# One statistics series and one transpose for two token blocks, two earlier broadcasts, and an earlier first split, in a linear-attention and MLP kernel

## The chip, the cores and the metric

The kernel runs on one core of a Trainium2 chip, as one program. The metric is the time of one execution on the device in microseconds (us); lower is better. All times below are of that core.

## What is computed

2048 tokens of width 640 go through a layer norm and then, side by side, through an attention and an MLP; both results are added to the input.

```python
def _layernorm(x, axis=-1, eps=1e-5):
    m = jnp.mean(x, axis=axis, keepdims=True)
    v = jnp.var(x, axis=axis, keepdims=True)
    return (x - m) / jnp.sqrt(v + eps)

def _A_ref(x, wqkv, w_phi, wo):            # 32 heads of 20
    qkv = (x @ wqkv) ...                    # q, k, v per head
    pq = jnp.einsum("bhsd,hdf->bhsf", q, w_phi)
    pk = jnp.einsum("bhsd,hdf->bhsf", k, w_phi)
    phi_q = jnp.concatenate([_softmax(pq), _softmax(-pq)], axis=-1)
    phi_k = jnp.concatenate([_softmax(pk), _softmax(-pk)], axis=-1)
    kv = jnp.einsum("bhsf,bhsd->bhfd", phi_k, v)
    z  = jnp.einsum("bhsf->bhf", phi_k)
    num = jnp.einsum("bhqf,bhfd->bhqd", phi_q, kv)
    den = jnp.einsum("bhqf,bhf->bhq", phi_q, z)[..., None] + 1e-6
    return (num / den) ... @ wo

def _B_ref(x, w1, b1, w2, b2):             # hidden width 1728
    y = _layernorm(x, axis=-1)
    h = _gelu(jnp.einsum("bsd,df->bsf", y, w1) + b1)
    return jnp.einsum("bsf,fd->bsd", h, w2) + b2

x = A_x
xn = _layernorm(x, axis=-1)
return x + _A_ref(xn, A_wqkv, A_w_phi, A_wo) + _B_ref(xn, B_w1, B_b1, B_w2, B_b2)
```

## The kernel before, in words

Every float32 operand of a matmul is split into a high and a low part (`split`, lines 53 and 54: ACT makes the high part by a copy, DVE or POOL subtracts it to get the low part), and a product is three matmuls (`mm3`, lines 60 to 62). The tokens are four blocks b of 512. The hidden width of the MLP is 14 chunks of 128, taken two at a time in seven groups g.

**A pass of the MLP** is one group for one block: `first` makes one hidden chunk by five `mm3` into a bank of the accumulator memory (banks 0, 1, 2 in turn), followed by the gelu (L242, ACT) and the split of its result (ACT L53, DVE L54, tile `m`). Then come five output chunks: ten matmuls or so each, into banks 5, 6, 7 in turn, each added to the tile `acc` by DVE (L286 in the first group, L288 after). Passes overlap by one: the two `first` of a pass stand ahead of the five output chunks of the pass before. Since three banks go round, an output chunk may start only when DVE has added up the chunk three places before it.

**Background work.** All else is written as Python generators that hang on `mlp.beside`: after each `mm3` (about 0.68 us of PE) one `next` lets the generator place a little more. So a count of `yield`s is a distance in PE's order. PE, DVE, ACT and POOL keep the order in which the program is written out in this part; the DMA issues on SP are ordered by a scheduler, and SP issues one after the other, waiting at each until its buffer or source is ready. The generator that matters here is `prep` (from line 448), which runs beside passes of blocks 0 and 1:

- twelve jobs of `prep_fold` (matmuls at L426 into banks 3 and 4 in turn, then a split) fold the feature map into the weights of k and q; six `yield`s each;
- among the jobs, `more_stats` (L434) makes mean and scale of the later tokens' eight tiles of 128: a tile `t` is loaded (L443, two buffers), two BN_STATS and a BN_AGGR on DVE (L126, L127), and after four tiles some small operations (L133 to L147) with one square root on ACT (L139), whose function table is loaded before it and gelu's again after it. On every second `yield` of a job, one step;
- five loads of v's weights (L465, buffers `raw`, two) with a split of each (tiles `wkh`, `wkl`);
- for b = 2 and then b = 3: `rows` (L166) copies the block's means and scales into `sc` (L169, L170), PE transposes it into 8 rows (L174), DVE copies that out (L176), it is stored to DRAM (L177) and read back as a broadcast to all partitions into the tile `m5` (L179, 512 KB). Then, five times, a piece of x (L478, buffer `raw`): POOL subtracts the mean (L488), DVE multiplies with the scale (L491), ACT makes the high part (L495), DVE the low part (L498), and both are stored (L500).

**The attention's end.** In the last group (g = 6) `first_split` (L931) splits the first block's attention output, `at[0].split` (ACT L914, DVE L916), for the output projection (L1020). It starts beside the pass (6, 3), after three empty `yield`s, and places one of its six steps per `yield`. The second chunk of group 6 is narrower and is built from halves: ACT L267, DVE L268, ACT L269 and L270, POOL L271.

## Time and profile before

| what | value |
|---|---|
| median of the runs; lowest | 741.25 us; 740.52 us |
| the profiled execution; its span | 740.65 us; 738.9 us |
| granted clock of TensorE | 1.000 |
| PE busy | 717.3 us, 97% of the span |
| DVE, ACT, POOL busy | 480.5, 314.4, 370.5 us |
| DMA, mean over the span | 129 GB/s |

In the rows of a timeline stand the start from the span's begin, the duration, engine, line, operation, the tiles written and read, the shapes, the count, and in brackets how long the engine had been idle before and what ended that. PE rows overlap: a matmul of 512 columns starts every 0.23 us and is shown 0.39 us long, so the bracket counts from a modelled end. In the chain of waits each piece is start, length, and what was waited for. In a table of windows the columns are the stretch, its length, the busy time of PE, PE's weight loads, DVE, ACT and POOL, the granted clock, the DMA share and GB/s.

### The profile page before, as it was taken

What the parts mean: (1) busy time and instruction counts of PE and PEld (TensorE: products, weight loads), DVE (VectorE), ACT (ScalarE), POOL (GpSimd) and SP (SyncE); (2) the same over time, 40 slices, a digit from 0 to 9 for tenths busy, and PEclk for the clock granted to TensorE, in tenths of its full rate; (3) what the DMA queues carried; (4) which work ended last, traced back from release to release, by engine and by line L of the source; (5) the groups of instructions that cost most, each with busy time, mean ns of one, the idle gap of its engine ahead of it and who ended that gap; (6) DMA issues with size and microseconds to landing.
All of it is one profiled execution on the core that took longest, in us unless ns stands there. A gap on an engine that the chain in (4) does not pass through costs nothing.

```text
span 738.9 us, 9634 instructions
## 1 busy us (share of the span) xinstructions
PE 717.3 (97%) x3423; PEld 606.6 (82%) x3423; DVE 480.5 (65%) x790; ACT 314.4 (43%) x518; POOL 370.5 (50%) x321
## 2 busy tenths in 40 slices
PE   4999999998999999999999999999999999999998
PEld 4888788777788998998998888888878888877886
DVE  7846744565653888888878788635565656766331
ACT  3614434333332455455345456246555556440110
POOL 1501222343321797697778889446576777304000
PEclk9999999999999999999999999999999999999999
DMA  9604467465543124634600705753433453153222
GB/s 333 214 8 121 146 170 183 133 198 149 166 167 142 64 80 161 149 101 161 143 0 1 179 0 200 179 162 111 125 110 115 118 154 92 48 209 129 86 84 73
DMA packets 64520, 95.36 MB, mean 129 GB/s; under 512 B 13312, under 2 KB 35216, under 8 KB 62848
## 3 DMA queue, kind: packets, MB, share of 16 engines
q1 hardware_dynamic: 64184, 94.74, 42.5%
q8 instruction: 27, 0.44, 0.2%
q14 instruction: 21, 0.17, 0.1%
q10 hardware_dynamic: 288, 0.01, 0.0%
HBM read 64.47 MB, written 30.26 MB: 128 GB/s over the span
## 4 chain that ended last, share of the span: by engine, by line
PE 79%; DVE 8%; DMA 5%; ACT 2%; issue 2%; POOL 2%; SPq 0%; POOLq 0%; DVEq 0%
PE bank L60 23%; PE bank L62 23%; PE bank L61 23%; PE bank L629 2%; PE bank L426 2%; PE bank L852 1%; PE bank L851 1%; DVE st L126 1%; DMA m<-r 1%; DVE y L916 1%; DMA raw<-in_wv 1%; DVE acc L288 1%; DVE xb L150 1%; POOL w L54 1%; POOL raw L488 1%
## 5 line engine op out<-in xcount | busy, mean ns | idle before, releaser
L54 POOL TENSOR_TENSOR w<-r,w 128x640 fp32r<-128x640 f32 x52 | 83.6, 1626 | 110.5 <-ACT w L53 104.6
L60 PE MATMUL bank<-y,w 128*128 128x512 f32 (+1 forms) x334 | 131.1, 392 | 0.9 <-ACT m L242 0.5
L62 PE MATMUL bank<-y,w 128*128 128x512 f32 (+1 forms) x334 | 129.8, 388 | 0.0
L61 PE MATMUL bank<-y,w 128*128 128x512 f32 (+1 forms) x334 | 129.6, 388 | 0.0
L60 PE MATMUL bank<-m,w 128*128 128x512 f32 x260 | 104.2, 401 | 4.2 <-DVE acc L288 3.9
L62 PE MATMUL bank<-m,w 128*128 128x512 f32 x260 | 101.9, 392 | 0.0
L61 PE MATMUL bank<-m,w 128*128 128x512 f32 x260 | 101.7, 391 | 0.0
L288 DVE TENSOR_TENSOR acc<-bank,acc 128x512 f32<-128x512 f32 x120 | 80.5, 681 | 16.5 <-PE bank L62 10.9
L60 PE MATMUL bank<-wkh,y 128*128 128x456 f32 (+2 forms) x240 | 88.6, 369 | 0.0
L61 PE MATMUL bank<-wkl,y 128*128 128x456 f32 (+2 forms) x240 | 88.5, 369 | 0.0
L62 PE MATMUL bank<-wkh,y 128*128 128x456 f32 (+2 forms) x240 | 88.4, 368 | 0.0
L54 DVE TENSOR_TENSOR m<-m,m 128x512 fp32r<-128x512 f32 (+1 forms) x54 | 42.7, 790 | 68.4 <-ACT m L53 68.4
L60 PEld LDWEIGHTS bank<-y,w 128*128 128x128 f32 x334 | 62.8, 188 | 14.1 <-DVE ob L1020 0.8
L62 PEld LDWEIGHTS bank<-y,w 128*128 128x128 f32 x334 | 62.7, 188 | 13.5 <-POOL w L54 0.4
L61 PEld LDWEIGHTS bank<-y,w 128*128 128x128 f32 x334 | 62.8, 188 | 12.7
L598 POOL TENSOR_TENSOR m<-m,mx 128x640 f32<-128x640 f32 (+2 forms) x48 | 44.4, 939 | 46.4 <-DVE mx L587 46.4
L580 ACT ACTIVATE m<-bank 128x456 f32<-128x456 f32 (+3 forms) x64 | 27.0, 421 | 95.0 <-PE bank L62 78.5
L60 PEld LDWEIGHTS bank<-m,w 128*128 128x128 f32 x260 | 48.9, 188 | 17.5 <-DVE acc L288 6.8
L845 POOL TENSOR_TENSOR e<-e,m 120x512 fp32r<-120x512 f32 (+1 forms) x28 | 38.0, 1358 | 43.0 <-ACT m L844 42.4
L62 PEld LDWEIGHTS bank<-m,w 128*128 128x128 f32 x260 | 48.8, 188 | 10.5
L601 DVE TENSOR_REDUCE sm<-m 128x64 f32<-128x1280 f32 x32 | 47.2, 1476 | 15.6 <-ACT m L599 15.5
L61 PEld LDWEIGHTS bank<-m,w 128*128 128x128 f32 x260 | 48.9, 188 | 9.6
(149 smaller groups left out, 1383.9 us busy)
## 6 DMA issues: line engine op xcount, KB each, us to landing
r<-in_w SPq DMA_DIRECT2D x52, 320.0 KB
e<-e SPq DMA_DIRECT2D x40, 240.0 KB
e<-acc SPq DMA_DIRECT2D x52, 160.0 KB
acc<-in_xT SPq DMA_DIRECT2D x4, 1280.0 KB
xb<-in_x SPq DMA_DIRECT2D x8, 320.0 KB
t<-in_x SPq DMA_DIRECT2D x8, 320.0 KB
raw<-in_xT SPq DMA_DIRECT2D x10, 256.0 KB
yh<-t SPq DMA_DIRECT2D x10, 256.0 KB
```

Source lines behind the costliest of these rows:

```text
L54: eng.tensor_tensor(lo, src, f(hi), op=ALU.subtract)
L60: nc.tensor.matmul(ps, lh, rh, start=first, stop=False, **kw)
L61: nc.tensor.matmul(ps, lh, rl, start=False, stop=False, **kw)
L62: nc.tensor.matmul(ps, ll, rh, start=False, stop=last, **kw)
L126: nc.vector.bn_stats(st[:, i, h, :], xb[:, h * 320:(h + 1) * 320])
L288: nc.vector.tensor_tensor(acc[b][:, m, :], pw, acc[b][:, m, :], op=ALU.add)
L426: nc.tensor.matmul(ps[:, i * kd:(i + 1) * kd], raw[:kk, (k + i) * P:(k + i + 1) * P], wpt[:kk, g, :kd // DF, 1:], start=True, stop=True)
L580: return nc.scalar.activation(p3[:, h:h + src.shape[1], 1:], src, AF.Copy).ins
L598: subs[n, t] = nc.gpsimd.tensor_tensor(ep[:, s], a, b, op=ALU.subtract)
L601: nc.vector.tensor_reduce(sm, e.rearrange("p s (h f) -> p (s h) f", f=DH), axis=AX, op=ALU.add)
L629: nc.tensor.matmul(kvp[g // 2][:VM, (g % 2) * 240:(g % 2) * 240 + 240].rearrange("p (s f) -> p s f", s=4), v[:, g * VS:g * VS + VM], ft[:, ...
L845: nc.gpsimd.tensor_tensor(pl, e, f(ph), op=ALU.subtract)
```

## The change

Four edits, all in generators beside the MLP. First, `more_stats` runs the eight later tiles as one series, with one square root, on every third `yield` of a job instead of every second. Second, `rows` is part of that series: the means and scales of both blocks go into one `sc` of 16 columns, with one transpose, one copy and one store. Third, the broadcast read is a function of its own, `load_rows`: for b = 2 it stands beside v's first load, for b = 3 at that block's start; the empty `yield`s ahead of the pieces become 5 and 10 (they were 2 and 7 for each block). Fourth, `first_split` loses its three empty `yield`s and places two steps per `yield`.

```diff
-    r_dram = [tc.dram_tile([8, P], F32, name=f"r{b}") for b in range(NB)]
+    r_dram = tc.dram_tile([2, 8, P], F32, name="r")
...
-    def rows(b, xp, ptile):
-
-        sc = xp.tile([P, 2, 4], F32, name="sc", bufs=1)
-        nc.vector.tensor_copy(sc[:, 0, :], mv[:, 4 * b:4 * b + 4, 0])
-        nc.vector.tensor_copy(sc[:, 1, :], ry[:, 4 * b:4 * b + 4])
-        for _ in range(2):
+    def rows(xp, ptile):
+
+        sc = xp.tile([P, 2, 2, 4], F32, name="sc", bufs=1)
+        for a, src in enumerate((mv[:, 8:16, 0], ry[:, 8:16])):
+            nc.vector.tensor_copy(sc[:, :, a, :], src.rearrange("p (b t) -> p b t", b=2))
+        for _ in range(5):
             yield
         ps = ptile()
-        nc.tensor.transpose(ps[:8, :P], sc.rearrange("p a t -> p (a t)"), idt)
-        sr = xp.tile([8, P], F32, name="sr8", bufs=1)
-        nc.vector.tensor_copy(sr, ps[:8, :P])
-        nc.sync.dma_start(r_dram[b], sr)
+        nc.tensor.transpose(ps[:16, :P], sc.rearrange("p b a t -> p (b a t)"), idt)
+        sr = xp.tile([16, P], F32, name="sr16", bufs=1)
+        nc.vector.tensor_copy(sr, ps[:16, :P])
+        nc.sync.dma_start(r_dram.rearrange("b r t -> (b r) t"), sr)
+
+    def load_rows(b):
+
         mr = mtile(5)
         nc.sync.dma_start(mr.rearrange("p a t -> p (a t)"),
-                          r_dram[b].rearrange("r t -> (r t)").unsqueeze(0).to_broadcast([P, 8 * P]))
+                          r_dram[b - 2].rearrange("r t -> (r t)").unsqueeze(0).to_broadcast([P, 8 * P]))
         return mr
...
     def more_stats():
 
-        for b in range(2, 4):
-            def tiles():
-                xbs = {}
-                for t in (*range(4 * b, 4 * b + 4), None):
-                    if t is not None:
-                        xbs[t] = fp.tile([P, 2, KC, G5], F32, name="t").rearrange("p a c f -> p (a c f)")[:, :D]
-                        nc.sync.dma_start(xbs[t], x[t * P:(t + 1) * P, :])
-                    if xbs and t != 4 * b:
-                        yield xbs.pop(min(xbs))
-            yield from stats(range(4 * b, 4 * b + 4), fp, tiles())
+        def tiles():
+            xbs = {}
+            for t in (*range(8, 16), None):
+                if t is not None:
+                    xbs[t] = fp.tile([P, 2, KC, G5], F32, name="t").rearrange("p a c f -> p (a c f)")[:, :D]
+                    nc.sync.dma_start(xbs[t], x[t * P:(t + 1) * P, :])
+                if xbs and t != 8:
+                    yield xbs.pop(min(xbs))
+        yield from stats(range(8, 16), fp, tiles())
+        for _ in range(2):
+            yield
+        yield from rows(fp, mlp.px)
...
-                if i > 0 and k % 2:
+                if i > 0 and k % 3 == 1:
                     next(more, None)
                 yield
...
+        for _ in more:
+            yield
         ahead = load_v(0)
+        mr = load_rows(2)
...
         for b in range(2, 4):
-            mr = yield from rows(b, fp, mlp.px)
             ahead = load(b, 0)
-            for _ in range(7):
+            if b == 3:
+                mr = load_rows(3)
+            for _ in range(5 if b == 2 else 10):
                 yield
...
     def first_split():
-        for i in range(3):
-            yield
         for c in range(KC + 1):
             at[0].split(c, nc.vector)
-            yield
+            if c % 2:
+                yield
```

How the order moves at three places of DVE, whose order is as written. The first is the ten output chunks of the two passes beside the jobs of k (`st` and `mv` are the statistics, `acc1` the sums of block 1, `bank5` to `bank7` the output banks, `wkl` a job's low part). Before:

```order
L286 SCALAR_TENSOR_TENSOR acc1_103<-bank6_723,b2t_61,acc1_103 128x512
L140 RECIPROCAL rr_746<-sr_745 128x8
L141 TENSOR_TENSOR rr_746<-rr_746,q_734 128x8
L142 TENSOR_TENSOR sr_745<-sr_745,rr_746 128x8
L143 RECIPROCAL ry_63<-sr_745 128x4
L286 SCALAR_TENSOR_TENSOR acc1_103<-bank7_738,b2t_61,acc1_103 128x512
L54 TENSOR_TENSOR wkl_593<-bank3_768,wkh_592 128x4x114
L146 RECIPROCAL ra_778<-sr_745 128x4
L147 TENSOR_TENSOR rs_all_64<-sr_745,ra_778 128x4
L126 BN_STATS st_781<-t_782 128x6 x2
L127 BN_AGGR mv_62<-st_781 128x2
L288 TENSOR_TENSOR acc1_103<-bank5_762,acc1_103 128x512
```

Changed:

```order
L289 SCALAR_TENSOR_TENSOR acc1_100<-bank6_717,b2t_61,acc1_100 128x512
L126 BN_STATS st_659<-t_711 128x6 x2
L127 BN_AGGR mv_62<-st_659 128x2
L289 SCALAR_TENSOR_TENSOR acc1_100<-bank7_729,b2t_61,acc1_100 128x512
L54 TENSOR_TENSOR wkl_590<-bank3_757,wkh_589 128x4x114
L126 BN_STATS st_659<-t_733 128x6 x2
L127 BN_AGGR mv_62<-st_659 128x2
L291 TENSOR_TENSOR acc1_100<-bank5_751,acc1_100 128x512
L54 TENSOR_TENSOR wkl_590<-bank4_780,wkh_589 128x114
L291 TENSOR_TENSOR acc1_100<-bank6_773,acc1_100 128x512
```

The small operations have left this stretch (they now stand behind the tenth chunk), and at most one tile's statistics stands between two sums.

The second place is behind v's last split (`wkl<-raw`), where the sums of block 0 (`acc0`) start; `m2` is the low part of a hidden chunk. Before:

```order
L54 TENSOR_TENSOR wkl_593<-raw_1237,wkh_592 128x640
L169 COPY sc_1266<-mv_62 128x4
L170 COPY sc_1266<-ry_63 128x4
L54 TENSOR_TENSOR m2_1245<-m4_1216,m2_1245 128x512
L176 COPY sr8_1281<-bank3_1279 8x128
L288 TENSOR_TENSOR acc0_102<-bank5_1272,acc0_102 128x512
```

Changed:

```order
L54 TENSOR_TENSOR wkl_590<-raw_1230,wkh_589 128x640
L54 TENSOR_TENSOR m2_1238<-m4_1209,m2_1238 128x512
L291 TENSOR_TENSOR acc0_99<-bank5_1264,acc0_99 128x512
L291 TENSOR_TENSOR acc0_99<-bank6_1272,acc0_99 128x512
L291 TENSOR_TENSOR acc0_99<-bank7_1280,acc0_99 128x512
L500 TENSOR_TENSOR raw_1259<-raw_1259,m5_1172 128x512
```

The copies into `sc` and the one out of the transpose's bank are gone from here, and the first piece of x for b = 2 comes two sums earlier.

The third place is the attention's first split (`y10<-ob0`) in group 6; `acc2` and `acc3` are the sums of blocks 2 and 3, `m4` the narrow chunk. Before:

```order
L288 TENSOR_TENSOR acc3_4089<-bank7_5799,acc3_4089 128x512
L916 TENSOR_TENSOR y10_5832<-ob0_4346,y00_5831 128x512
L54 TENSOR_TENSOR m1_5816<-m4_5815,m1_5816 128x512
L268 TENSOR_TENSOR m4_5815<-bank2_5844,m4_5815 64x512
L916 TENSOR_TENSOR y10_5832<-ob0_4346,y00_5831 128x512
L288 TENSOR_TENSOR acc2_4088<-bank5_5860,acc2_4088 128x512
L916 TENSOR_TENSOR y10_5832<-ob0_4346,y00_5831 128x512
L288 TENSOR_TENSOR acc2_4088<-bank6_5870,acc2_4088 128x512
```

Changed:

```order
L291 TENSOR_TENSOR acc3_4064<-bank7_5774,acc3_4064 128x512
L925 TENSOR_TENSOR y10_5797<-ob0_4321,y00_5796 128x512 x5
L54 TENSOR_TENSOR m1_5791<-m4_5790,m1_5791 128x512
L271 TENSOR_TENSOR m4_5790<-bank2_5828,m4_5790 64x512
L291 TENSOR_TENSOR acc2_4063<-bank5_5844,acc2_4063 128x512
L291 TENSOR_TENSOR acc2_4063<-bank6_5852,acc2_4063 128x512
```

All five low parts now stand ahead of the hidden chunk's, and none between the sums; on ACT the five high parts stand ahead of that chunk's gelu in the same way.

On SP two things move: the broadcast for b = 2 is issued just ahead of v's first load (it stood behind the first two loads of x's pieces), and the one for b = 3 stands ahead of the last stores of b = 2, where it waits for DVE's last multiplication with the old `m5`. On PE one transpose of the two is left, between two `mm3` of the tenth job.

## The prediction

> **What bounds the kernel now.** I read the table of windows first, to see whether PE has idle time at all and where.
>
> ```profile
> 60.00:90.00 30.00, 29.09 (x152) 23.79 (x151) 23.20 (x62) 11.92 (x23) 6.18 (x4) 1.00 0.55 161
> ...
> 126.00:150.00 24.00, 22.79 (x101) 18.25 (x100) 14.95 (x21) 9.78 (x15) 8.44 (x6) 1.00 0.50 156
> 150.00:200.00 50.00, 47.31 (x206) 37.95 (x205) 30.67 (x46) 16.99 (x27) 21.30 (x14) 1.00 0.58 171
> 200.00:640.00 440.00, 439.07 (x2108) 377.69 (x2108) 311.06 (x473) 218.89 (x350) 303.51 (x275) 1.00 0.39 115
> 640.00:680.00 40.00, 38.75 (x170) 31.16 (x169) 27.88 (x43) 10.96 (x19) 10.08 (x7) 1.00 0.40 143
> ```
>
> PE sets the pace: in the 440 us from 200 to 640 it is idle for 0.93 us, and its clock is granted in full in every row. What is left to win lies in 60 to 90 (0.91 us idle), 126 to 200 (1.21 + 2.69) and 640 to 680 (1.25), which are the places that the change touches. PE's timeline shows these stalls one by one; for the largest, I keep its neighbours.
>
> ```profile
> 70.53 0.47 PE L60 MATMUL bank<-m,w 128*128 128x512 f32 x1 [0.23 <-DVE acc L286]
> 76.72 0.50 PE L60 MATMUL bank<-m,w 128*128 128x512 f32 x1 [0.68 <-DVE acc L288]
> 132.26 0.39 PE L62 MATMUL bank<-m,w 128*128 128x512 f32 x1
> 133.83 0.27 PE L174 MATMUL bank<-idt,sc 128*8 128x128 f32 x1 [1.19 <-DVE sc L170]
> 134.17 0.40 PE L61 MATMUL bank<-m,w 128*128 128x512 f32 x1
> 164.73 0.50 PE L60 MATMUL bank<-m,w 128*128 128x512 f32 x1 [0.34 <-DVE acc L288]
> 168.74 0.27 PE L174 MATMUL bank<-idt,sc 128*8 128x128 f32 x1 [0.32 <-DVE sc L170]
> 178.63 0.39 PE L61 MATMUL bank<-m,w 128*128 128x512 f32 x1
> 178.85 0.39 PE L62 MATMUL bank<-m,w 128*128 128x512 f32 x1
> 180.87 0.50 PE L60 MATMUL bank<-m,w 128*128 128x512 f32 x1 [1.63 <-DVE acc L288]
> 181.21 0.40 PE L61 MATMUL bank<-m,w 128*128 128x512 f32 x1
> 195.15 0.50 PE L60 MATMUL bank<-m,w 128*128 128x512 f32 x1 [0.39 <-DVE acc L288]
> 659.27 0.50 PE L60 MATMUL bank<-m,w 128*128 128x512 f32 x1 [0.87 <-DVE acc L288]
> 677.10 0.50 PE L60 MATMUL bank<-y,w 128*128 128x512 f32 x1 [0.38 <-DVE ob L1020]
> ```
>
> The bracket understates a stall, since matmuls overlap. Undisturbed, they start 0.225 us apart (178.63 to 178.85). From 178.85 to 181.21 are two steps, 2.36 us in place of 0.45: a loss of 1.91 for an idle time of 1.63. So a stall costs its bracket plus 0.28; 132.26 to 134.17 gives the same (1.46 against 1.19 + 0.28). The losses are then 0.51, 0.96, 1.47, 0.62, 0.60, 1.91, 0.67, 1.15 and 0.66: 8.55 us, of which the change can reach all but the last, 7.9. That is 1.1% of the time, so whatever happens here stays within the 2% (14.8 us) that a measurement of this kernel can tell from no change.
>
> **The change part by part. The statistics.**
>
> ```profile
> 66.44 0.89 DVE L126 BATCH_NORM_STATS2 st<-t 128x6 f32<-128x320 f32 x2 [0.45 <-DMA t<-in_x]
> ...
> 73.73 1.35 DVE L147 TENSOR_TENSOR rs_all<-sr,ra 128x4 f32<-128x4 f32 x1
> ...
> 76.03 0.64 DVE L288 TENSOR_TENSOR acc<-bank,acc 128x512 f32<-128x512 f32 x1
> ```
>
> Ten output chunks stand here in a row, three to a stretch of two jobs' halves, about 5.3 us of PE. DVE's part of such a stretch is three sums (0.6 each), a job's low parts (0.9) and, before, three tiles' statistics (1.05 each with the BN_AGGR): 5.85 us, more than PE takes, plus waits for the tile's load and the small operations in between. With two tiles' statistics it is 4.8 us. A sum may be late by two chunks, some 3.5 us, so DVE then keeps up and both stalls go: 1.47. I take 1.2 (bounds: 1.47, and 0.5 if only the first goes), because one of the later x tiles' loads now stands on SP behind weight loads that wait for POOL and can come late by a microsecond; a sum behind it has two chunks to spare, the low parts of the next job have less. One square root for two saves a handful of operations of 0.16 to 0.2 us on DVE, which nothing waits for.
>
> ```profile
> 69.22 1.28 ACT L139 ACT_TABLE_LOAD   x1
> ...
> 101.44 0.68 DVE L288 TENSOR_TENSOR acc<-bank,acc 128x512 f32<-128x512 f32 x1
> ```
>
> The table load moves, it does not go: there are two as before. One, 1.28 us, now stands ahead of a gelu near 90 us. That hidden chunk is first used by the pass whose sums start at 101.44, so ten microseconds hide it; without that cover it would cost its 1.28.
>
> **The transpose.**
>
> ```profile
> 132.71 0.82 DVE L54 TENSOR_TENSOR wkl<-raw,wkh 128x640 fp32r<-128x640 f32 x1 [1.02 <-ACT wkh L53]
> ...
> 133.53 0.16 DVE L170 COPY sc<-ry 128x4 f32<-128x4 f32 x1
> ...
> 134.76 0.67 DVE L288 TENSOR_TENSOR acc<-bank,acc 128x512 f32<-128x512 f32 x1
> ```
>
> PE stood at 133.83 because `sc` waits in DVE's order behind v's last split, which waits for ACT and that for a DMA. In the changed order the copies into `sc` stand five `yield`s' steps, over ten microseconds, ahead of the transpose, so this wait goes. What is late next: the first sum, at 134.76. Without the copy out of the transpose it starts at about 134.6 and ends at 135.25, while PE, not held up, wants its bank three chunks (18 steps, 4.08 us) after this pass's first matmul at 131.13 (132.26 is the sixth), at 135.2. So a wait of about 0.1 with its 0.28 stays: of 1.47 I take 1.1 (bounds: 1.47, and 0.5 if v's loads come 0.6 later). The second transpose's 0.60 goes; the one that is left costs 133.83 to 134.17 less one step, 0.11, at another place: 0.5 in sum.
>
> ```profile
> 113.15 0.33 SPq L465 DMA_DIRECT2D raw<-in_wv  x1
> ...
> 118.94 0.73 ACT L53 ACTIVATE wkh<-raw 128x640 fp32r<-128x640 f32 x1
> ...
> 172.16 4.56 DMA m<-r
> ```
>
> The broadcast is issued ahead of v's first load. That load has 5.8 us until its split. If it had to wait for a whole broadcast, the 4.56 us from issue to landing in this chain of waits, on top of about 3 for itself, it would come some 2 us late, and the DVE half of that split stands behind three sums until 122 us, which hides it. Cost nothing; two microseconds on ACT if it does not hide.
>
> **The broadcasts of x's pieces.**
>
> ```profile
> 164.59 0.68 DVE raw L491
> ...
> 169.41 2.73 DMA r<-sr
> ...
> 178.39 1.28 POOL raw L488
> ```
>
> ```profile
> 178.46 1.75 DVE L491 TENSOR_TENSOR raw<-raw,m 128x512 f32<-128x512 f32 x1 [1.18 <-POOL raw L488]
> 180.14 1.27 DVE L288 TENSOR_TENSOR acc<-bank,acc 128x512 f32<-128x512 f32 x2
> ```
>
> For b = 3 the store and the read back take 2.73 + 4.56 = 7.3 us behind the transpose; POOL can only then subtract, DVE's multiplication waits, and behind it stand the two sums that PE waits for at 180.87. Now the store is done 50 us ahead, and the read is issued when the last multiplication of b = 2 has freed the old `m5`. That one runs at 164.59 now, so even with no gain ahead of it the broadcast lands by 165.3 + 4.6 = 169.9, seven us before it does today. The 1.91 goes whole (bounds: 1.91, and 0.6 if a held multiplication still adds a microsecond there, as 178.46 shows). For b = 2 the pieces start some 4 us sooner, so that DVE's work on the fourth piece no longer falls late ahead of the sum that PE waits for at 164.73: of 0.62 I take 0.5. The stall at 195.15 comes from a low part that met a POOL operation; such a meeting moves rather than goes, and of 0.67 I take 0.3 (bounds for the two: all 1.29, or a loss of 0.6 if a pass that is free today gets such a meeting).
>
> **The first split.**
>
> ```profile
> 651.69 0.69 ACT L242 ACTIVATE m<-bank,b1t 128x512 f32<-128x512 f32 x1 [6.49 <-PE bank L62]
> ...
> 656.60 4.26 ACT L914 ACTIVATE y<-ob 128x512 fp32r<-128x512 f32 x8
> ```
>
> ```profile
> 657.25 1.36 DVE L916 TENSOR_TENSOR y<-ob,y 128x512 fp32r<-128x512 f32 x1 [0.78 <-ACT y L914]
> 658.53 0.68 DVE L288 TENSOR_TENSOR acc<-bank,acc 128x512 f32<-128x512 f32 x1
> ```
>
> The third high part stands on ACT behind the narrow chunk's last copy, so DVE's low part waits for it 0.78 us, and the second sum behind it comes at 658.53, which is PE's stall at 659.27. Now ACT makes all five (0.53 each) in the 6.49 us that it idles ahead of the gelu at 651.69, and DVE the five low parts, 0.6 each, behind the last sum of the pass before, ahead of 652; the gelu's own low part is not due before 653 (651.69 + 0.69 + 0.63 for the copy). Were that gap not there, the five would put the gelu off by 2.7 us. The second sum then comes at about 656.4. Of 1.15 I take 1.1 (bounds: 1.15 and 0.6, if the second sum is late by half of what it is now). What follows (the shuffles and low parts up to 677) hangs in DVE's order behind sums that PE paces, so it moves with PE and its 0.66 stays.
>
> **The sum.** 1.2 + 1.1 + 0.5 + 0.5 + 1.9 + 0.3 + 1.1 = 6.6, less 0.4 for meetings of DVE and POOL at new places: 6.2. From the profiled execution's own 740.65 that gives 734.5 us. It lies 0.6 below the median of the runs, so against that it is 0.9%.
>
> **The rivals.** First, a wait takes the place of the one removed: v's five splits are a chain of loads into two buffers, and PE, which now arrives 1.5 us earlier, stands at the first sum behind them, or the late x tile keeps one of the first two stalls. Then 1.0 is lost of the 1.2, 0.8 of the 1.6, and another 0.9 where the pieces of x follow v's loads: 737.2. For it speaks the 0.1 us margin above; against it that the broadcast has left the place where those loads run.
>
> Second, the stalls merely move on: if the background is itself the limit between 120 and 200, PE waits as long as before, a little later. Only 1.2 and 1.1 stay: 738.4. Against it, DVE is busy for 30.67 us of the 50 and POOL for 21.30.
>
> Third, slower than before: DVE and POOL hold each other up.
>
> ```profile
> 71.95 3.10 POOL L54 TENSOR_TENSOR w<-r,w 128x640 fp32r<-128x640 f32 x2 [35.43 <-ACT w L53]
> ```
>
> The tiny operation at 73.73 lasts 1.35 us and ends at 75.08, just where POOL's pair ends (75.05). Pieces that start earlier could meet POOL ahead of the first sum of each pass. That sum has about 1.4 us to spare (0.8 with a piece's operation ahead of it). Two held operations, each lengthened by up to 1.2 (the excess at 73.73), make 2.4 - 0.8 + 0.28, about 1.9 us a pass. Of my 6.2, the 2.7 of the three sum stalls (164 to 195) would go with it, leaving 3.5; so two of the five passes with pieces make it slower than before, and three give 740.65 - 3.5 + 5.7 = 742.9. For it speak 178.46 (1.75 in place of 0.68); against it, that it takes two such meetings in one pass, which only one of today's stalls (164.73) comes near. The Trainium skill has this as a rule (SBUF — State Buffer, "SBUF: two separate sides"): VectorE and GpSimd share a pair of ports, taken as a whole by whichever instruction starts first, and an operation of DVE with two inputs from SBUF waits for all of a GpSimd instruction that reads SBUF. The end at 75.08 agrees with it; by the rule every meeting costs the rest of POOL's operation, which is this rival, while by the rows most operations pass untouched.
>
> **How the numbers follow.** The forecast has 0.70, the first rival 0.16, the second 0.07, the slower one 0.04; 0.03 is left for more than forecast (all 7.9 and some of the last stall: 732.2). The predicted time is 734.5. The range reaches from 732.0 to 738.2, which leaves out most of the second rival and the slower one. The cases all lie within 2%: faster by more than that would need 14.8 us where PE idles 7; slower by as much needs more held passes than there are. Faster 0.01, same 0.98, slower 0.01.
>
> **What would show it.** PE's waits for `sc` are gone; no wait of 1 us for `acc` near 180; the wait at 659 is gone and the one at 677 stays near 0.4; 60 to 90 and 126 to 200 show PE idle for less than 1.2 us together; PE's span elsewhere is unchanged. Wrong would be a new wait of PE behind v's splits, DVE waiting for `t<-in_x` again with a bank wait behind it, or multiplications L500 of 1.5 us and more ahead of a first sum.

## The result and the profile after

The changed kernel takes 734.13 us (median of six runs, 732.96 to 736.36), the kernel before beside it 741.02 (median of six): a ratio of 0.9911, 95% interval 0.990 to 0.9921, so 0.9% faster. Forecast were 734.5 and a range of 732.0 to 738.2. The profiled execution took 732.96 us with a span of 731.2 (before: 740.65 and 738.9); it is the fastest of the six, which matters below. Three single runs were disturbed (891.73 and 3005.81 of the kernel before, 1022.29 of the kernel with the broadcast behind v's third load, at a granted clock of 0.66): the ratios leave them out, the medians given do not, and without them 741.02 would be 740.8 and that later kernel's 733.0 would be 732.63.

The table of windows of the changed kernel, cut at the same times (columns: the stretch, its length, then busy time and instructions of PE, its weight loads, DVE, ACT and POOL, granted clock, share of the DMA engines, GB/s; the share counts a packet's whole time where it starts, so it can pass 1):

```profile
60.00:90.00 30.00, 30.00 (x159) 25.10 (x158) 21.18 (x55) 12.22 (x22) 6.17 (x4) 1.00 0.54 159
...
126.00:150.00 24.00, 23.49 (x104) 19.10 (x103) 15.53 (x21) 10.44 (x16) 9.07 (x7) 1.00 0.53 169
150.00:200.00 50.00, 50.00 (x222) 41.42 (x221) 30.70 (x46) 20.10 (x32) 20.73 (x15) 1.00 0.57 169
200.00:640.00 440.00, 439.03 (x2109) 377.60 (x2108) 309.53 (x470) 220.01 (x353) 302.87 (x274) 1.00 0.39 115
640.00:680.00 40.00, 39.63 (x175) 32.51 (x174) 26.87 (x42) 9.14 (x17) 8.80 (x6) 1.00 0.48 169
```

PE's idle time is now 0.00 in 60 to 90 (0.91 before), 0.51 and 0.00 in 126 to 200 (1.21 and 2.69), and 0.37 in 640 to 680 (1.25). The 440 us between have 0.97 against 0.93: the rest of the kernel is as it was. PE's timeline of the changed kernel shows the two stalls that these numbers stand for:

```profile
134.45 0.50 PE L60 MATMUL bank<-m,w 128*128 128x512 f32 x1 [0.51 <-DVE acc L291]
...
669.53 0.50 PE L60 MATMUL bank<-y,w 128*128 128x512 f32 x1 [0.37 <-DVE ob L1028]
```

Eight stalls have gone, one is new (134.45), and the one that the change could not reach is still there (677.10 before, 0.38). With 0.28 for each stall beside its bracket, the eight cost 0.51 + 0.96 + 1.47 + 0.62 + 0.60 + 1.91 + 0.67 + 1.15 = 7.89, the new one 0.51 + 0.28 = 0.79, and the transpose that is left 0.1: 7.0 of the 7.7 by which the span fell. Of the other 0.7, some 0.3 lies in the first and last microseconds, which the change does not touch; 0.4 I can't place.

The new stall's chain of waits in the changed kernel (start, length, what; each line was waited for by the next, and pieces called issue, of 0.02 to 0.04 us, are left out):

```profile
120.98 0.83 DVE wkl L54
121.83 4.74 DMA raw<-in_wv
126.59 0.75 ACT wkh L53
127.36 0.84 DVE wkl L54
128.22 2.85 DMA raw<-in_wv
131.09 0.74 ACT wkh L53
131.83 0.59 ACT m L245
132.44 0.64 ACT m L53
133.10 0.69 DVE m L54
133.80 0.61 DVE acc L291
134.45 0.50 PE bank L60
```

This is the chain of v's loads through two buffers: v's first split on DVE frees a buffer, the third load lands 4.74 us after its issue, its split frees the buffer for the fifth load, and behind that load's high part stand, on ACT, the gelu and high part of a hidden chunk, whose low part DVE makes just ahead of its first sum. In the kernel before, the same load took 3.93 us. This difference is what the later experiments look into.

### The profile page after: what moved, and what is told of

It is laid out like the page before. It is cut to its first block, busy times and chain, and to the rows that moved or that the text cites. A ratio compares the mean times of both kernels' runs of the same rounds, so it can differ in the third digit from the quotient of the medians.

```text
span 731.2 us, 9616 instructions
## 1 busy us (share of the span) xinstructions
PE 714.9 (98%) x3422; PEld 607.0 (83%) x3422; DVE 474.4 (65%) x779; ACT 314.9 (43%) x517; POOL 370.1 (51%) x321
## 4 chain that ended last, share of the span: by engine, by line
PE 84%; DVE 8%; POOL 2%; DMA 2%; ACT 2%; issue 1%; SPq 1%; DVEq 0%; POOLq 0%; ACTq 0%
PE bank L60 25%; PE bank L61 25%; PE bank L62 25%; PE bank L429 2%; PE bank L638 2%; POOL m L607 2%; PE bank L861 1%; PE bank L860 1%; DMA raw<-in_wv 1%; SPq L671 1%; DVE st L126 1%; DVE y L925 1%; DVE xb L150 1%; POOL m L618 1%; PE bank L268 1%
## 5 line engine op out<-in xcount | busy, mean ns | idle before, releaser
L245 ACT ACTIVATE m<-bank,b1t 128x512 f32<-128x512 f32 (+1 forms) x54 | 36.1, 671 | 53.6 <-PE bank L62 52.5
L60 PEld LDWEIGHTS bank<-m,w 128*128 128x128 f32 x260 | 48.9, 188 | 11.7 <-DVE acc L291 1.8
L62 PEld LDWEIGHTS bank<-m,w 128*128 128x128 f32 x260 | 48.8, 188 | 10.5
```

What stands on the lines that cost most here:

```text
L60: nc.tensor.matmul(ps, lh, rh, start=first, stop=False, **kw)
L62: nc.tensor.matmul(ps, ll, rh, start=False, stop=last, **kw)
L245: nc.scalar.activation(gt[:, cols], pz, AF.Gelu_apprx_tanh, bias=b1t[:, 2 * g + j:2 * g + j + 1])
```

## The experiments

Each kernel is shown as a difference to the changed kernel, or to the kernel before where that is said. The kernel before, run on the same chips, had medians of 741.14 to 741.35.

**The statistics' pace, alone.** The kernel before with one line changed.

```
-                if i > 0 and k % 2:
+                if i > 0 and k % 3 == 1:
```

> The kernel before with one edit: the statistics step on every third yield of a job instead of every second; two series, two transposes, two stores and reads as before. Theory (each stall its own cause): the waits at 70 and 77 us go (0.23 and 0.68 us idle, 1.47 us of time); the waits for the transposes and the one of 1.6 us near 180 stay within 0.3 us; 1.2 to 1.5 us under the kernel before. Rival (DVE's relief in the first part is what lets all that follows run on time): the later waits shrink by half or more as well, 3 us or more under the kernel before.

Measured: 739.38 us, ratio 0.9973 (0.9963 to 0.9984); PE's stalls at 70 and 77 are gone, and all later ones are still there (1.45 for `sc`, 1.63 at 180, 0.87 at 658 among them). So the later stalls don't hang on this one, and none of them shrinks: two are larger than before (1.45 in place of 1.19, and 0.54 in place of 0.34 at 163.83) and one of 0.25 for `w` is new (142.33). The edit gave 2.0 by the medians (1.2 to 2.7 by the interval) and 0.9 by the profiled spans, against my 1.2.

**The pace, undone.** The changed kernel with `k % 2`, everything else kept.

> The changed kernel with the statistics at every second yield again, as before the change, but in their one series. This tests the step of my prediction that the two stalls at 70 and 77 us go because DVE has one tile's statistics less per stretch of three output chunks (4.8 us in place of 5.85, against PE's 5.3). Theory: the pace is the cause; PE waits for sums between 60 and 90 come back, 0.5 to 1.0 us in one or two, and the time is 0.8 to 1.5 above the changed kernel's 734.1. Rival: what counted was that the square root, the reciprocals and the second table load no longer stand in this stretch; then 60 to 90 stays free of waits and the time is that of the changed kernel.

Measured: 735.95 us, ratio 0.9929 (0.991 to 0.9948), 1.8 above the changed kernel where 0.8 to 1.5 was expected. PE's timeline of this kernel between 60 and 90:

```profile
70.48 0.47 PE L60 MATMUL bank<-m,w 128*128 128x512 f32 x1 [0.29 <-DVE acc L289]
75.42 0.50 PE L60 MATMUL bank<-m,w 128*128 128x512 f32 x1 [0.82 <-DVE acc L289]
77.55 0.50 PE L60 MATMUL bank<-m,w 128*128 128x512 f32 x1 [0.46 <-DVE acc L291]
```

And DVE's, ahead of the second:

```profile
70.44 0.87 DVE L126 BATCH_NORM_STATS2 st<-t 128x6 f32<-128x320 f32 x2
71.34 0.21 DVE L127 BATCH_NORM_AGGREGATE mv<-st 128x2 f32<-128x12 f32 x1
71.47 0.70 DVE L289 SCALAR_TENSOR_TENSOR acc<-bank,b2t,acc 128x512 f32<-128x512 f32 x1
73.62 0.89 DVE L126 BATCH_NORM_STATS2 st<-t 128x6 f32<-128x320 f32 x2 [1.45 <-DMA t<-in_x]
74.54 0.21 DVE L127 BATCH_NORM_AGGREGATE mv<-st 128x2 f32<-128x12 f32 x1
74.67 0.70 DVE L289 SCALAR_TENSOR_TENSOR acc<-bank,b2t,acc 128x512 f32<-128x512 f32 x1
```

The stalls are back, 0.29 + 0.82 + 0.46 and 0.28 each, 2.4 us. The rival, that the square root's small operations were the cause, has fallen: in this kernel they stand behind the last of the three stalls (from 79.24 on). But the second stall shows that it is not DVE's sum of work alone. The statistics also arrive ahead of their tiles, and 1.45 us of waiting for `t<-in_x` stands in DVE's order ahead of the sum that PE needs. The slower pace cures both: in the changed kernel the only such wait is 0.31 (at 78.51), with no stall behind it. A second thing differs in this kernel: the statistics are done sooner, so b = 2's broadcast is issued at 96.13, 18.5 us ahead of v's first load (114.64), and PE waits 0.02 us behind v's last split. That will matter below.

**The first split, alone.** The kernel before with the new `first_split`.

```
-        for i in range(3):
-            yield
         for c in range(KC + 1):
             at[0].split(c, nc.vector)
-            yield
+            if c % 2:
+                yield
```

> The kernel before with the new first split alone. Theory (every stall has its own cause, and their losses add): only the wait of PE at 659 us goes, 0.87 us idle and 1.15 us of time, and the five others of 0.23 to 1.63 us between 70 and 196 us stay as they are; the time is 1.0 to 1.3 us under the kernel before. Rival (the early part frees the late one, the first split is hidden anyway): no difference, 0 to 0.3 us.

Measured: 739.7 us, ratio 0.9984 (0.997 to 0.9999). The stall at 659 is gone, all others remain; 1.6 by the medians (0.1 to 2.2 by the interval), against 1.15 that the stall cost. This agrees with terms that add up, but the interval is wide, and the profiled execution (743.14) is the slowest of the ten, with two waits that the profile before lacks (0.46 at 145.83, 1.43 at 423.32).

**The broadcast for b = 3, late.** The changed kernel, its means and scales for b = 3 stored and read back only in place, by a copy on DVE six yields behind the first load of x (the lines of `load_rows` that make this copy, store and read are left out here); the pieces start after 14 yields. The control has the early broadcast and the same 14 yields.

```
             if b == 3:
-                mr = load_rows(3)
-            for _ in range(5 if b == 2 else 10):
+                for _ in range(6):
+                    yield
+                mr = load_rows(3, late=True)
+            for _ in range(5 if b == 2 else 8):
```

> The changed kernel, but the store and the broadcast read of block 3's means and scales hang on an extra small copy on DVE six yields into the block, and its pieces start after 14 yields instead of 10, so that copy, sums and the first multiplication stand in the order that the kernel before has there. Theory (the wait near 180 us came from the store and read of 7.3 us): PE waits again for a sum, 1.0 to 1.7 us idle near 173 us, 1.3 to 2.0 us more than the same with an early read. Rival (it is the place of the first multiplication ahead of the sums, and not the read, that made the wait): no more than 0.3 us over the control with 14 yields.

> Control for the late read: the changed kernel with 14 yields instead of 10 ahead of block 3's pieces, broadcast early as in the change. Theory: the multiplication finds its operand, no wait of over 0.5 us near 173 us, time within 0.7 us of the changed kernel. Rival (the place alone makes the wait): 1.0 to 1.7 us idle there and 1.3 to 2.0 us over the changed kernel.

Measured: 736.03 us (ratio 0.9925, 0.9901 to 0.995) with the late broadcast, 734.71 (0.9913, 0.989 to 0.9935) for the control. The late one's timelines of POOL, DVE and PE at that place:

```profile
173.26 3.02 POOL L508 TENSOR_TENSOR raw<-raw,m 128x512 f32<-128x512 f32 x2 [7.56 <-DMA m<-rlate]
```

```profile
175.05 1.78 DVE L511 TENSOR_TENSOR raw<-raw,m 128x512 f32<-128x512 f32 x1
```

```profile
177.48 0.50 PE L60 MATMUL bank<-m,w 128*128 128x512 f32 x1 [0.39 <-DVE acc L300]
```

POOL waits 7.56 us for the broadcast, and the stall is back; the control has none between 150 and 190. So a late broadcast does make a stall there, but not of the size expected: 0.39 instead of 1.0 to 1.7 of idle time. The multiplication was not late here but only long, 1.78 us in place of 0.69, beside POOL's second subtraction. In the kernel before it was both: 1.75 us long, after DVE had waited 1.18 for POOL's piece (the row at 178.46 in the prediction). The 1.63 there is about 0.39 and 1.18 together; that the lateness gave the larger part is read from this row and was not put back by a run. The other half of the 1.3 between the two medians is elsewhere: in the profiled runs PE waits behind v's last split for 2.04 us in the one and 1.37 in the other, though nothing in the program ahead of that place differs. The third load of v had taken 6.25 and 5.63 us. This is what made me doubt the sentence that the broadcast ahead of v's loads costs nothing.

**The broadcast for b = 2, late.** The same edit for b = 2, so that nothing is broadcast ahead of v's loads.

> The changed kernel, except that b = 2's means and scales are stored once more and read back only behind v's last split (an extra 16 x 128 copy on DVE, 4 KB stored, then the 512 KB broadcast), so that nothing is broadcast ahead of v's loads. Disputed is my prediction's sentence that the broadcast ahead of v's loads costs nothing. First theory (the broadcast slows the loads): v's third load, issued near 121.8 us, lands after 3.9 to 4.2 us as in the kernel before, not after 4.74 to 6.25 as in the three kernels with the broadcast there, and PE's wait for the first sum behind v's last split is below 0.3 us instead of 0.5 to 2.0. Second theory (the loads are slow for another reason, such as the stores of wq's parts or a load of x ahead of them): that load takes 4.7 us and more and the wait stays at 0.5 or more. In both, b = 2's pieces start some 7 us later, which by the earlier trial on b = 3 costs one wait of about 0.4 (0.7 with its 0.28). Time: 733.0 to 734.5 by the first theory, 734.5 to 736 by the second.

Measured: 738.76 us, ratio 0.9969 (0.9958 to 0.998). v's third load took 3.86 us and PE waited only 0.11 us behind v's last split: what the first theory says of the loads holds. The price of the lateness, though, I had far too low. The timelines of this kernel for POOL, ACT and PE:

```profile
140.95 1.29 POOL L504 TENSOR_TENSOR raw<-raw,m 128x512 f32<-128x512 f32 x1 [12.17 <-DMA m<-rlate]
```

```profile
143.01 0.63 ACT L511 ACTIVATE t<-raw 128x512 fp32r<-128x512 f32 x1 [8.53 <-DVE raw L507]
143.54 1.35 ACT L53 ACTIVATE w<-r 128x640 fp32r<-128x640 f32 x2
```

```profile
144.31 0.50 PE L60 MATMUL bank<-y,w 128*128 128x512 f32 x1 [2.02 <-ACT w L53]
146.23 0.50 PE L62 MATMUL bank<-y,w 128*128 128x512 f32 x1 [1.18 <-POOL w L54]
```

The piece waits for the broadcast, ACT's copy of the piece waits for the piece, and behind that copy in ACT's order stand the high parts of the next weights. PE waits for these, 2.02 and then 1.18 with 0.28 for each. The kernel before, whose broadcast landed at nearly the same time (140.47 against 140.83) but whose pieces start after seven yields in place of five, has no such wait in its profile (the kernels with one part alone have 0.25 and 0.46 for `w`). So the shorter lead of the changed kernel seems to work only because the broadcast is there by then; the late read with seven yields was not run. (Another 1.8 us were lost in the profiled run ahead of 40 us, where the kernels don't differ; so the time itself says less than the rows.)

**The broadcast behind v's third and last load.** Here it stays one transfer, and its place among v's loads changes. To hold it back until then, DVE sets one number of its target to zero, an operation of 0.06 us.

```
         mr = mtile(5)
+        if b == 2:
+            nc.vector.memset(mr[:1, 0, :1], 0.0)
...
         ahead = load_v(0)
-        mr = load_rows(2)
         for kc in range(KC):
             raw, ahead = ahead, load_v(kc + 1) if kc < KC - 1 else None
+            if kc == 3:
+                mr = load_rows(2)
```

(`kc == 1` for the other.)

> The changed kernel with b = 2's broadcast moved from ahead of v's first load to just behind the third (one number of its target is set to zero on DVE there, which only serves to hold the transfer back until then; nothing of the result changes). What the last trial left open: with the broadcast 20 us later, v's third load took 3.86 us, but the pieces came too late. First theory (a broadcast among v's loads slows whichever load runs beside it): loads one to three now land as before the change (the first split's high part starts without a wait for its load, the third load takes 3.7 to 4.2 us), and the fourth or fifth, issued beside the broadcast, takes 1 us longer; PE's wait behind v's last split is 0 to 0.9, so the time is within 0.7 of the changed kernel's 734.1. Second theory (only the first loads matter, since the chain makes up for what comes later): the wait is gone, 733.3. Third (the loads are slow for another reason): third load above 4.7 again, wait 0.5 to 2, 734 to 735.5.

> The same with the broadcast behind v's last load (issued near 128.5 us, ahead of the loads of x's pieces, which land at 134.3 in the changed kernel). If the broadcast is what slows v's loads, all five now take what they took before the change, PE's wait behind v's last split is 0 to 0.3, and POOL's first subtraction, which needs the broadcast by 134.3, starts less than 1.5 us later than there: 733.3 to 733.7 us, with less spread than the changed kernel's 733.0 to 736.4. If the subtraction comes later than the pair on the weights of the next group (137.68), that pair waits behind it and PE for the weights, as in the trial with b = 2 late: 735 to 738.

Measured: behind the third load 733.0 us, ratio 0.9884 (0.9868 to 0.9901), with the execution of 1022.29 us as its only profile, so its theories on the single loads are untested. Behind the last load 732.6 us, ratio 0.9885 (0.987 to 0.990): three of its four runs lie between 732.42 and 732.77, and the profiled one, at 733.99, has a 1.4 us wait at another place (L641, 0.3 in the changed kernel). The median is 1.5 below the changed kernel's and 0.7 below the lowest time expected. The third load took 3.81 us, and PE's timeline marks no stall between 60 and 200: of the 0.51 us behind v's last split 0.09 is left. POOL's first subtraction starts at 134.24 (134.30 in the changed kernel). ACT's first high part of v in the changed kernel, and with the broadcast behind v's last load:

```profile
119.45 0.74 ACT L53 ACTIVATE wkh<-raw 128x640 fp32r<-128x640 f32 x1 [1.82 <-DMA raw<-in_wv]
```

```profile
117.89 0.73 ACT L53 ACTIVATE wkh<-raw 128x640 fp32r<-128x640 f32 x1
```

The first waited 1.82 us for its load, the second not at all. In SP's order that load stands behind the broadcast, and was issued at 113.79 in place of 112.04. The chain's third load with the broadcast behind v's last load:

```profile
122.19 3.81 DMA raw<-in_wv
```

The shares of the DMA engines in the windows from 118 us on, changed kernel first:

```profile
118.00:122.00 4.00, 4.00 (x20) 3.28 (x19) 2.80 (x5) 0.74 (x1) 0.00 (x0) 1.00 1.16 248
122.00:126.00 4.00, 4.00 (x19) 3.34 (x18) 2.11 (x3) 2.06 (x3) 2.72 (x2) 1.00 0.59 96
```

and with the broadcast behind v's last load:

```profile
118.00:122.00 4.00, 4.00 (x19) 3.29 (x18) 2.79 (x6) 0.61 (x1) 0.00 (x0) 1.00 0.67 132
122.00:126.00 4.00, 4.00 (x20) 3.30 (x19) 2.52 (x4) 2.00 (x3) 2.36 (x2) 1.00 0.32 88
```

The broadcast is issued at 113.4, yet the load that suffers is issued at 121.8: the stores of wq's parts, which stand between them, are pushed back, and fill the DMA engines (1.16 against 0.67) when the third load starts. Their pieces are packets of under 512 bytes, 640 to a store, and the four stores issued from 114 to 119 us make 2560 of the 2686 such packets that the changed kernel starts from 114 to 126. It starts 285 of them by 118 us and 2209 from 118 to 122; with the broadcast behind v's last load it is 1334 and 1339, so the first two stores are out of the way by 118 there. Over the profiled runs of kernels that keep the order of v's loads, the two numbers go together (waits under 0.15 us are not marked in the timeline and are read from PE's busy time):

| kernel | third load of v, us | PE's wait behind v's last split |
|---|---|---|
| broadcast behind the last load | 3.81 | 0.09 |
| b = 2 late | 3.86 | 0.11 |
| pace undone (broadcast at 96.13) | 4.1 | 0.02 |
| both steps together (below) | 4.19 | 0.07 |
| changed kernel | 4.74 | 0.51 |
| second split later (below) | 5.09 | 1.25 |
| control with 14 yields | 5.63 | 1.37 |
| subtractions on DVE (below) | 5.64 | 1.38 |
| b = 3 late | 6.25 | 2.04 |

The first four have no broadcast just ahead of v's loads, the others have one. (4.1 is the time from the load's issue at 124.78 to the start of its split at 128.94.) The kernels with the old order have none either, and PE's wait for `sc` there goes the same way: 3.93 and 1.19 before, 4.06 and 1.26 with the split alone, 4.51 and 1.45 with the pace alone. So the slowest load without a broadcast (4.51) is only 0.2 us under the fastest with one (4.74): the broadcast is a cause, and something else moves this load by up to a microsecond and more, with one profile for each kernel. What that is stays open.

**v's loads two ahead.** The changed kernel, v's third and fourth load into the buffers `t`.

> The changed kernel, with v's loads issued two ahead of their splits in place of one (the third and fourth go into the buffers that the x tiles of the statistics have left). Theory: the wait that is left behind v's last split (0.51 in the changed kernel, 1.37 and 2.04 in two kernels that differ only behind it) is the chain of v's loads through two buffers; with two ahead no split waits for its load, DVE's last low part of v comes over 1 us earlier, the wait near 134.5 goes, and the time is 0.8 to 1.3 below the changed kernel's 734.1 (732.8 to 733.4; ratio to the kernel before 0.988 to 0.990). Rival: the chain is bound by ACT's and DVE's own order (a high part behind a copy, a low part behind three sums); then the splits no longer wait for loads, but the last low part comes as late as before and the wait of 0.5 stays: 734.1. A third way: the loads side by side slow each other and the first split comes late: 734.5 or more.

Measured: 733.68 us, ratio 0.9902 (0.9887 to 0.9916), with a wait of 0.90 left behind v's last split. It does not decide, because the edit did not do what it says: the buffers `t` were still being stored from. The chain of waits of this kernel:

```profile
118.36 8.31 DMA wql<-t
126.73 3.26 DMA t<-in_wv
```

The fourth load was issued only when a store of wq's part had landed, 8.31 us after its issue. What it adds is the time that this store took.

**The subtractions on DVE.** The changed kernel, with `nc.vector` in place of `nc.gpsimd` in the subtraction of the mean from x's pieces.

> The changed kernel, with the ten subtractions of x's pieces (b = 2 and 3) on DVE instead of POOL. This tests the rival that DVE and POOL hold each other up. In the changed kernel five operations of DVE between 138 and 183 us last 1.2 to 1.8 instead of 0.6 to 0.7, each ending about 0.6 us behind the end of an operation of POOL. If POOL's subtractions are what holds them, these five fall to the one or two that meet POOL's pairs on weights (138.12 and perhaps one more), and DVE's busy time there grows by ten times 0.68 less some four times 0.8, so about 3.6 us. As none of the five made PE wait, the time stays within 0.7 of the changed kernel's 734.1. If, against that, the holds had cost PE time in some other way, it falls by 0.5 to 1; if DVE has no room for ten more operations, a first sum of a pass comes late and one or two waits of 0.3 to 0.7 appear: 735 to 736.

Measured: 733.76 us, ratio 0.9914 (0.9892 to 0.9936), as the changed kernel. DVE's busy time grew by 6.8 (474.4 to 481.2, ten times 0.68), not 3.6, because the number of long operations hardly fell: four in place of five. They meet POOL's pairs on the weights now. DVE and POOL in this kernel:

```profile
139.56 2.05 DVE L497 TENSOR_TENSOR raw<-raw,m 128x512 f32<-128x512 f32 x1
```

```profile
139.00 4.04 POOL L54 TENSOR_TENSOR w<-r,w 128x640 fp32r<-128x640 f32 x2 [12.66 <-ACT w L53]
```

So taking one kind of POOL's work away doesn't end the meetings, and in neither kernel does one of these reach PE.

**The second split later.** The changed kernel, for the stall that neither kernel had lost.

```
-                    for n, at_ in enumerate((3, 28, 53), 1):
+                    for n, at_ in enumerate((10, 28, 53), 1):
```

> The changed kernel, with the attention's second split (block 1) starting at step 10 of the output projection in place of 3. It goes for the stall that the change left standing, 0.38 before and 0.37 after, which I counted as 0.66 and put down to DVE's order: the low parts of the second split stand between the shuffles, where POOL's operation meets them. Theory: with the split seven steps later the low parts no longer stand ahead of the copy of ob that PE waits for near 669.5; the wait goes and the time falls by 0.66 to about 733.5 (ratio 0.990). Rival: the copy is late for its own reason (the shuffle ahead of it), and the wait stays at 0.3 to 0.5; or the low parts come too late for the next stage, with a new wait of PE for the attention's input of 0.5 or more: 734.1 to 735.

Measured: 733.46 us, ratio 0.9902 (0.9885 to 0.9918); the wait for `ob` near 670 is gone, with PE busy for all of 640 to 680. The times alone can't tell this kernel from the changed one (the intervals overlap), and the span (731.6) hides the gain, since this run had the 1.25 behind v's last split. What DVE and POOL do there in the changed kernel,

```profile
660.99 3.15 DVE L925 TENSOR_TENSOR y<-ob,y 128x512 fp32r<-128x512 f32 x2
...
665.29 2.36 DVE L925 TENSOR_TENSOR y<-ob,y 128x512 fp32r<-128x512 f32 x2
```

```profile
659.34 4.24 POOL L906 TENSOR_TENSOR acc<-acc,rx 128x512 f32<-128x512 f32 x3 [7.51 <-DVE rx L904]
```

and DVE with the split seven steps later:

```profile
667.47 3.09 DVE L925 TENSOR_TENSOR y<-ob,y 128x512 fp32r<-128x512 f32 x5
```

Five low parts take 3.09 us when POOL is idle, two take 3.15 beside POOL's sums. Here, then, DVE and POOL holding each other up seems to stop PE: the pair at 665.29 lasts 1.1 us more than two alone (1.24), and the copy of `ob` behind it came 0.37 too late. The run moved the low parts as a whole, though, so that it is their length and not their mere place is read from these rows. (The Trainium skill, SBUF — State Buffer, "SBUF: two separate sides", has DVE's operation with two inputs from SBUF wait for all of a GpSimd instruction that reads SBUF and has started first. These rows agree: each low part takes about as long as one of POOL's sums.)

**Both steps.** The broadcast behind v's last load and the later second split.

> The changed kernel with both single steps that took a wait away: b = 2's broadcast behind v's last load, and the attention's second split at step 10 of the output projection in place of 3. Theory: what the two save adds up, as the waits have causes of their own: no wait of PE for a sum between 60 and 200 us, none for ob near 670, so 0.79 (0.51 + 0.28, and more against runs where that wait was 1.3 or 2) and 0.65 (0.37 + 0.28) below the changed kernel's 734.1: 731.9 to 732.7, ratio to the kernel before 0.987 to 0.989, and less spread. Rival: both save in the spread only, or the wait for ob comes back when PE arrives at another moment against POOL: 733.0 or more.

Measured: 732.77 us (731.8 to 734.55), ratio 0.9889 (0.9871 to 0.9907). In the profiled execution (731.89, span 730.1, the shortest of those profiled) PE's timeline marks no stall between 60 and 200 and none near 670, as expected; but the median is only that of the broadcast's move alone, and the spread has not shrunk. So the stalls add up in the trace, not in the times. What makes three of the five runs 0.9 to 2.7 us longer, the profile of the fast one can't show.

## Why the prediction was right, step by step

**The bound.** PE sets the pace and nothing outside the stalls was to be had: right, the 440 us are unchanged and the gain is the stalls'. That a stall costs its bracket plus 0.28 was not tested by itself; it accounts for 7.0 of 7.7.

**The statistics,** 1.2: the trace gives all of it, 1.47, the upper bound. The reason was half of it, by the undone pace: DVE has less to do per stretch, and it also no longer stands waiting for a tile, a wait that the prediction names beside its 5.85 us but gives no size.

**The transpose,** 1.1 and 0.5: the second is right (0.60 less 0.1). The first is the term that was too large, 1.47 - 0.79 = 0.68 in the profiled run, which is the fastest of the six; with a third load of 5.6 to 6.3 us, as in other profiles, nothing of it or less than nothing is left (1.37 + 0.28 is more than 1.47). I had named the margin, 0.1 us, and the bound, 0.5 if v's loads come 0.6 later. The step that failed is the sentence on the broadcast, "Cost nothing". I had priced only the load that stands next to it, and that one was hidden as I said: the first high part waited 1.82 us, and DVE reached its low part at 120.98 all the same. What I left out is the stores behind it, through which it slows the third load, in a chain without slack: 4.74 us in place of 3.93, and a new wait of 0.51. "A new wait of PE behind v's splits" was one of my signs of being wrong, and it came. (The Trainium skill, DMA: Bandwidth & Descriptors, "Queues, rings and completion order", says that on each DMA engine the descriptors of one queue are consumed in the order of the ring. SP issues all of these transfers, so by this the 512 KB stand ahead of everything that SP issues behind them; the loads of 4.74 to 6.25 us and the late short packets agree with it. That order itself is not shown by a row here.) This is the first rival in part, by another cause than it gave: PE arriving sooner was worth no more than 0.11 us of idle time where the third load took 3.8 to 4.2. The margin itself was right, as PE's timeline shows for the kernel with the broadcast behind v's last load:

```profile
133.91 0.39 PE L62 MATMUL bank<-m,w 128*128 128x512 f32 x1
134.39 0.50 PE L60 MATMUL bank<-m,w 128*128 128x512 f32 x1
134.73 0.39 PE L61 MATMUL bank<-m,w 128*128 128x512 f32 x1
```

From 133.91 to 134.73 are two steps, 0.82 us in place of 0.45. These 0.37 are the 0.1 and its 0.28, and they leave 1.10 of the 1.47, the term that I had forecast for a broadcast without a price.

**The broadcasts of x's pieces,** 0.5, 1.9 and 0.3: 0.62, 1.91 and 0.67, all of them gone. For the middle one, putting a late read back brought a stall again, but a quarter of the old one; the rest is read from DVE's wait of 1.18 in the kernel before. Why the stall at 195 went whole was not tried; with the late broadcast, its control and either part alone there is one of 0.4 near 190 to 198, so it may depend on where POOL's operations fall.

**The first split,** 1.1: 1.15. The cover that I named was there. ACT and DVE of the changed kernel:

```profile
637.84 2.70 ACT L923 ACTIVATE y<-ob 128x512 fp32r<-128x512 f32 x5
...
645.46 0.69 ACT L245 ACTIVATE m<-bank,b1t 128x512 f32<-128x512 f32 x1 [4.92 <-PE bank L62]
```

```profile
642.61 3.09 DVE L925 TENSOR_TENSOR y<-ob,y 128x512 fp32r<-128x512 f32 x5
```

The gelu at 645.46 still waits 4.92 us for PE, so the five high parts put nothing off, and the low parts end at 645.70, ahead of its own low part.

**The meetings of DVE and POOL,** less 0.4: they came, five operations of DVE between 138 and 183 that last 1.2 to 1.8 us, and cost PE nothing. One is an L500 of 1.76 us (182.86), another of my signs of being wrong, with no stall behind it. The slower rival stands where it stood: each meeting costs DVE 0.5 to 1.1 us, but it needs one in front of an operation without slack. Only the late broadcast for b = 3 (0.39) and the second split (0.37) seem to have that.

The sum was 1.5 too small against the profiled execution (7.7 against 6.2): 0.3 from the statistics, 0.4 from the meetings that were free, 0.5 from two stalls that went whole, 0.7 from what I can't place or lies at the ends, less 0.4 from v's loads. Against the medians (741.02 to 734.13, 6.9) it is 0.7 too small, probably because the changed kernel's usual run has more of the wait for v's loads than the profiled one, its fastest; of the usual run there is no profile. So the mechanism was right in its main parts, and wrong in the price of the broadcast and in that of the meetings, while it is in part luck that 734.5 came within 0.4 us of the median: the errors of the terms, 1.2 and more on one side and 0.4 on the other, and the variable wait made up for each other.

## What to carry to other kernels

A transfer moved to an idle-looking place is not free if the queue behind it feeds a chain of loads through two buffers: look not at the load next to it but at every transfer issued in the following ten microseconds, and put it behind the last load of the chain if its reader allows. Before removing a wait, read how much room the next sum in order has; here 0.1 us of margin, not the cause of the old wait, set the new time. And where a stall goes, look at the engine orders that were tuned to it: here the pieces start two yields earlier than before, and once their broadcast came late again they held up the next weights (2.02 and 1.18 us).

## What the runs showed of the hardware

- A transfer slows one issued 8 us later: with a broadcast of 512 KB ahead, a load of 320 KB took 4.74 to 6.25 us from issue to landing (five kernels), without it 3.81 to 4.51 (seven kernels; 3.93 before the change). The spread between kernels with the same code up to that point (4.74 to 6.25) is larger than the gap between the groups.
- An operation of DVE beside one of POOL can be long, and so can POOL's: two low parts took 3.15 us in place of 1.24 (five took 3.09 alone). POOL's three sums took 4.24 with the low parts beside them and 3.79 without.
- A store of the last, narrow part of wq (95 KB by the table of issues) took 8.31 us to land in that stretch, so a buffer that it reads from is not free for a load for that long.
